# Twelve other weight blocks are streamed through four places, and the work tiles of a step are packed anew (attention with memory and a state space convolution, one core)

## The chip, the cores and the metric

The kernel runs on one core of a Trainium2 chip. The metric is the device time of one execution in microseconds. A kernel is timed in several runs and the median is given. A profile is one further execution with the hardware profiler on. Engines are named as the profile names them: PE (TensorE, matmuls), PEld (its weight loads), DVE (VectorE), ACT (ScalarE), POOL (GpSimd) and SP (SyncE, which here only issues transfers). A "q" behind an engine is its queue of issued transfers.

## The reference, cut to what matters

There are two parts, and the output joins them side by side. Part B is a convolution of a 2048 x 1024 input with kernels that come from a state space model. It runs first and the change does not touch its code. Part A is a recurrent attention over 64 segments of 32 rows, and each segment needs 8 rows of memory that the one before it wrote:

```python
mem = mem0
for s in range(n_seg):
    h = jnp.concatenate([mem, x[:, s * 32:(s + 1) * 32]], axis=1)
    q, k, v = (jnp.einsum('btd,dhe->bhte', h, W) for W in (Wq, Wk, Wv))
    scores = jnp.where(mask, jnp.einsum('bhqe,bhke->bhqk', q, k) * scale, -1e9)
    o = jnp.einsum('bhqk,bhke->bhqe', softmax(scores), v)
    o = jnp.einsum('bhte,hed->btd', o, Wo)
    mem = o[:, :8]
    outs.append(o[:, 8:])
```

Model width is 1024, with 32 heads of 128. So Wq, Wk, Wv and Wo have 1024 x 4096 elements each, in bf16, 8 MB a matrix, and every segment uses all of them.

## The kernel before

The loop over segments is a chain: the memory rows of one step enter the matmuls of the next. A step works with 32 rows, the 8 rows of memory and 24 rows of x ("hT", transposed). The projections of the other 8 rows of each segment do not depend on memory; they are made ahead of the loop, kept in HBM (PKd, PVd and VXd) and read in by each step (`load_pk`, line 327, and `load_vx`, line 333, which also brings the 24 rows of x of the next step).

**Weights.** The 32 MB of weights are cut in 64 blocks of 128 x 2048 elements, 0.5 MB each. A block is named by matrix, half of the heads and the slice of the contraction, such as ("v", 1, 5), or for Wo by a pair of heads, such as ("o", 9). The on-chip memory (SBUF) holds 49 of them for the whole loop ("resident"). Three ("kept": k 0 7, q 0 7, o 15) lie wholly or half in PSUM and are copied by DVE to SBUF work space in each step (`fetch`, line 292). The other twelve are listed in STREAM and STREAM_O (lines 25 and 26). They are copied once to HBM tiles of their own (WD) and are loaded again in every step, through four places ("wst") used in turn. `unit` (line 261) is called as PE's matmuls are written down: when it meets a streamed block, `stage` (line 294) issues the load on SP's queue to the next of the four places. That load waits until PE has used the block that was loaded four loads earlier. Resident blocks whose first use lies in the first step are loaded from the same queue as they are met.

**A step** in PE's order is: k half 0 (slices 0, 2, 4, 6, 1, 3, 5, 7), q half 0, k half 1 with the transposes of k0 and q0 and the first scores in between, q half 1, v half 0 with the transposes of k1 and q1 after three of its slices and the second scores at its end, v half 1 with the first part's weighted values (pv) after six slices, Wo 0 to 4, pv of the second half, Wo 5 to 15, and the transposes of the new memory rows. Line 365 is the projection matmul (four of 512 columns a block, in four row groups at once), 474 the one with Wo (eight of 256 columns), 376 the transposes, 390 and 394 the scores, 573 the transpose of the new memory, which DVE copies to hT (line 575).

ACT copies each projection from PSUM to SBUF (`evac`, line 371), fills the scores with the mask (384), takes Exp (410), and issues the loads of pk and vx and the two stores of a step's result (`stores`: line 343 to the scratch tensor OLd, 347 to the output). DVE does the softmax sums and the KT0 copy (489), POOL adds the columns of the precomputed keys to KT0 and KT1 (379).

**Work tiles.** All work tiles of a step lie in one SBUF tile, the arena, of 5984 bytes a partition, at byte offsets written by hand (AT, line 36). Tiles that overlap must not live at once. Where they do in part, the framework finds the overlap and puts in a wait: a writer waits for the last readers and writers of what it overwrites, and for a transfer's landing where that is one of them. A step's result ("ob", 1024 bytes) is written by ACT at the step's end, read by the two stores, and its place is written again by the next step. The order of the instructions on each engine is the order in which the program writes them; there is no scheduler in this part.

Of the kernel before, what the change touches and what calls it, by code (L numbers as in the profile page):

```python
# [21 lines left out]

STREAM = {("k", 0): (2, 3), ("q", 0): (4,), ("k", 1): (3,), ("q", 1): (4,), ("v", 0): (0, 6), ("v", 1): (1, 5)}
STREAM_O = (1, 5, 9)

BANK = {("k", 0): "b0", ("q", 0): "b1", ("k", 1): "b2", ("q", 1): "b0", ("v", 0): "b3", ("v", 1): "b2"}
KEPT = {("k", 0, 7): (("K7a", 0, 512), ("K7b", 512, 512), ("K7c", 1024, 512), ("K7d", 1536, 384), (None, 1920, 128)),
# [3 lines left out]
SLOTS = 4  # L33

ARENA = 5984
AT = {"K7a": 4960, "K7b": 2048, "K7c": 1024, "K7d": 3136, "ob": 3904, "pk": 0, "vx": 3392, "Q7a": 2048, "Q7b": 4960,
      "k0": 1024, "q0": 2048, "KT0": 4704, "QT0": 1024, "k1": 1024, "q1": 4288, "pn0": 5312, "pt0": 2304, "KT1": 1024,
      "QT1": 4288, "pb0": 4288, "V0": 1024, "L0": 5472, "o0": 2368, "V1": 1024, "pn1": 2048, "pt1": 4288, "pb1": 0,
      "lb1": 4960, "ln1": 320, "lt1": 0, "L1": 2048, "o1": 3904, "Oa": 4960, "Ob": 2560}


def weight_blocks(Wq, Wk, Wv, Wo):
# [15 lines left out]
def streamed_keys():  # L58
    return [key for key in [(m, t, kc) for (m, t), kcs in STREAM.items() for kc in kcs] + [("o", u) for u in STREAM_O]]

# [172 lines left out]
def part_a(ctx, tc, x, src, WD, HE, seg_len, out_a, ahead, W_res, rest, places, first):  # L233
# [25 lines left out]
    between = {}  # L259
# [22 lines left out]
    def at(name, *dims):  # L282

        n = int(np.prod(dims))
        t_ = arena[:, AT[name] // 2:AT[name] // 2 + n]
        if len(dims) == 1:
            return t_
        names = "abc"[:len(dims)]
        return t_.rearrange("p (%s) -> p %s" % (" ".join(names), " ".join(names)), **dict(zip(names, dims)))

    def words(out, in_):
        nc.vector.tensor_scalar(out=out.bitcast(I32), in0=in_.bitcast(I32), scalar1=0, scalar2=None, op0=ALU.bitwise_or)  # L292

    def stage(key, in_):
        t_ = wst.tile([128, 2048], BF16, name="wst", tag="w%d" % (loads[0] % SLOTS))
        loads[0] += 1
        nc.sync.dma_start(out=t_[:].rearrange("e (h d) -> e h d", h=2) if len(in_.shape) == 3 else t_[:], in_=in_)
        return t_

    def load_kept(key):  # L300
        t_ = first.pop(key) if key in first else stage(key, src(key))
        kept[key] = {}
        for n in (1,) if key in HALF else (0, 1):
            kept[key][n] = ps_k.tile([128, 512], F32, name="keep", tag="keep%d" % sum(len(b) for b in kept.values()))
            words(kept[key][n][:], t_[:, 1024 * n:1024 * n + 1024])
        if key in HALF:
            t_ = ahead.low["half"] if key[0] == "q" else wres.tile([128, 1024], BF16, name="Whalf")
            nc.sync.dma_start(out=t_[:], in_=src(key)[:, 0, :] if key[0] == "o" else src(key)[:, 0:1024])
            halves[key] = [(0, 1024, t_)]
# [15 lines left out]
    def load_pk(j):  # L325
        pk = at("pk", 512)
        nc.scalar.dma_start(out=pk, in_=PKd[j])
        return pk

    def load_vx(j):  # L330
        n = 448 if j + 1 < NS else 256
        vx = at("vx", 448)
        nc.scalar.dma_start(out=vx[:, 0:n], in_=VXd[j + 1, :, 0:n])
        return vx
# [17 lines left out]
    load_kept(("k", 0, 7))  # L352
    fetch(("k", 0, 7))
    pk = load_pk(0)
    between["q", 0, 4] = lambda: load_kept(("q", 0, 7))
    between["v", 0, 6] = lambda: load_kept(("o", 15))
    for s in range(NS):
        def quads(m, t, kcs, a=None):
# [10 lines left out]
        def evac(a, name):  # L369
            q = at(name, 512)  # L370
            nc.scalar.copy(out=q, in_=a[:])  # L371
            return q
# [39 lines left out]
        def weigh(sc, i, pn):  # L412
            x, m_ = flat(sc, i), maxima(i)
            nc.vector.tensor_reduce(out=m_, in_=x, axis=AX.X, op=ALU.add)  # L414
            nc.vector.reciprocal(out=m_, in_=m_)
            pn = at(pn, x.shape[1], NK)
            nc.vector.tensor_tensor(out=pn, in0=x, in1=bc(m_.unsqueeze(2), [128, x.shape[1], NK]), op=ALU.mult)
            return pn

        def turn(pn, pt):  # L420
            n = pn.shape[1]
            pt = at(pt, n + n // 4, SL)
            nc.vector.transpose(out=pt[:, 0:n, :], in_=pn[:, :, 0:SL])
            nc.vector.transpose(out=pt[:, n:n + n // 4, :], in_=pn[:, :, SL:NK])  # L424
            return pt
# [9 lines left out]
        def left_blocks(lt, lk, name):  # L435
            L = at(name, 2, 16, XL)
            nc.gpsimd.tensor_tensor(out=L[:, 0].rearrange("p (a b) k -> p a b k", a=4), in0=bc(lt[:, :, 0:XL].unsqueeze(2), [128, 4, 4, XL]),  # L437
                                    in1=bc(BD[:].unsqueeze(1).unsqueeze(3), [128, 4, 4, XL]), op=ALU.mult)
            spread_l(nc.gpsimd, L[:, 1], lk[:, 0:XL], 0, 16, XL)
            return L  # L440
# [17 lines left out]
        def evac_o(p, name):  # L458
            o = at(name, 4, 4, SL)
            nc.scalar.copy(out=o, in_=p[:].rearrange("p a (g q) -> p a g q", g=4))  # L460
            return o
# [16 lines left out]
        k0 = evac(a, "k0")  # L478
# [3 lines left out]
        q0 = evac(a, "q0")  # L482
# [5 lines left out]
        QT0, KT0 = at("QT0", 4, 4, SL), at("KT0", 4, 4, NK)  # L488
        nc.vector.tensor_copy(out=KT0[:, :, :, 0:SL], in_=pk_[:])  # L489
        nc.scalar.copy(out=QT0, in_=pq[:])  # L490
        vx = load_vx(s)
# [5 lines left out]
        k1 = evac(a, "k1")  # L497
# [3 lines left out]
        pt0 = turn(weigh(sc0, None, "pn0"), "pt0")  # L501
        q1 = evac(a, "q1")
# [5 lines left out]
        KT1, QT1 = at("KT1", 4, 4, NK), at("QT1", 4, 4, SL)  # L508
# [20 lines left out]
        pb0 = at("pb0", 4, 4, SL)  # L529
        spread(pb0, pt0[:, 0:4, :])  # L530
        L0 = left_blocks(pt0[:, 4:8, :], pt0[:, 9, :], "L0")
# [4 lines left out]
        V0 = evac(a, "V0")  # L536
# [7 lines left out]
        o0 = evac_o(pv0, "o0")  # L544
        pt1 = turn(weigh(sc1, 0, "pn1"), "pt1")
        pb1 = at("pb1", 4, 4, SL)
        spread(pb1, pt1[:, 0:4, :])
        lb1 = at("lb1", 512)
        spread_l(nc.vector, lb1.rearrange("p (a k) -> p a k", k=SL), pt1[:, 4, :], 0, 16, SL)
        quads("v", 1, range(6, KC), a)  # L550
        V1 = evac(a, "V1")
# [6 lines left out]
        o1 = evac_o(pv1, "o1")  # L558
        lt1 = turn(weigh(sc1, 1, "ln1"), "lt1")
        oproj(pp[:, 1, :], range(5, 8), o0)  # L560
        L1 = left_blocks(lt1[:, 0:4, :], lt1[:, 4, :], "L1")
        fetch(("o", 15))
        oproj(pp[:, 1, :], range(8, 16), o1)
        ob = at("ob", 2, 256)
# [14 lines left out]
        if s + 1 < NS:  # L579
            pk = load_pk(s + 1)  # L580
# [806 lines left out]
def kernel(  # L1387
# [92 lines left out]
    with ExitStack() as ctx_a:  # L1480
        part_a(ctx_a, tc, A_x[0], src, WD, A_Wo.shape[0] * A_Wo.shape[1], seg_len, out_a, ahead, W_res, rest, places, first)
# [35 lines left out]
```

## Time and profile before

| | us |
|---|---|
| median of 3 runs (lowest, highest) | 2136.48 (2134.81, 2144.58) |
| the profiled execution, its own time | 2141.16 |
| its span | 2139.4 |
| PE busy (share of the span) | 1885.6 (88%) |
| DVE busy | 1442.0 (67%) |
| ACT busy | 1045.2 (49%) |
| POOL busy | 435.8 (20%) |
| mean rate of transfers | 276 GB/s, 590.78 MB |
| streamed blocks, loads of 512 KB | 768 |

Times of the profile are microseconds from the span's start. A row of the page with digits cuts the span in 40 equal slices of 53.5 us, each digit the busy share in tenths. A wait is given as the waiting engine and line, and what released it. "L365 PE MATMUL acc<-wst,a_hT" is the matmul of line 365 that reads a streamed block, "acc<-W,a_hT" one with a resident block; "arena" is any work tile. In a timeline, a bracket at the end of a line is the idle time of the engine ahead of it and what ended that.

### The profile page before, as it was taken

How to read it: one execution, taken by the hardware profiler on the slowest of the kernel's cores; microseconds unless marked ns; L12 is line 12 of the kernel's file. 1: busy time of each engine (PE TensorE's matmuls, PEld its weight loads, DVE VectorE, ACT ScalarE, POOL GpSimd, SP SyncE). 2: the span in 40 equal slices, each digit the busy share in tenths (PEclk: the TensorE clock that was granted, in tenths of full speed). 3: DMA queues.
4: the chain of work that ended last, by engine and by line, in shares of the span. 5: the costliest groups of instructions: out<-in, count | busy, mean ns of one | idle time of the engine just before them, and what ended most of it. 6: DMA issues, size and time to landing. Idle time of an engine off the chain costs nothing. (4 is left out here: it accounts for less than half of the span.)

```text
span 2139.4 us, 78633 instructions
## 1 busy us (share of the span) xinstructions
PE 1885.6 (88%) x33734; PEld 1183.7 (55%) x33734; DVE 1442.0 (67%) x3353; ACT 1045.2 (49%) x1915; POOL 435.8 (20%) x780
## 2 busy tenths in 40 slices
PE   1589999977999779999999999999998998999999
PEld 1365656656888535555555555555554555555554
DVE  8589999989999246566566665666655565666650
ACT  6699999971333324444444444444434343444430
POOL 2145445452111101111111111111111111111121
PEclk9999999989999889999999999999999999999999
DMA  6767886556745899999999999999998999999991
GB/s 162 191 198 229 241 226 176 163 174 204 242 134 175 302 350 328 324 324 338 319 337 333 325 322 324 328 335 338 324 321 302 320 323 317 308 334 334 327 335 57
DMA packets 344019, 590.78 MB, mean 276 GB/s; under 512 B 108537, under 2 KB 220185, under 8 KB 341621
## 3 DMA queue, kind: packets, MB, share of 16 engines
q1 hardware_dynamic: 297016, 528.00, 74.1%
q0 software_dynamic: 10544, 33.69, 4.6%
q10 hardware_dynamic: 36108, 24.07, 3.7%
q8 instruction: 264, 4.33, 0.8%
q14 instruction: 87, 0.70, 0.1%
HBM read 530.86 MB, written 65.26 MB: 279 GB/s over the span
## 5 line engine op out<-in xcount | busy, mean ns | idle before, releaser
L365 PEld LDWEIGHTS <-a_hT 128*32 128x32 bf16 x12352 | 337.5, 96 | 326.5 <-issue 79.6
L371 ACT CAST arena<-acc 128x512 bf16<-128x512 f32 x384 | 224.9, 586 | 421.2 <-PE acc L365 274.6
L365 PE MATMUL acc<-W,a_hT 128*32 128x512 bf16 x4864 | 376.1, 383 | 0.0
L474 PEld LDWEIGHTS <-arena 128*32 128x32 bf16 x8256 | 211.2, 97 | 110.8 <-issue 54.1
L365 PE MATMUL acc<-wst,a_hT 128*32 128x512 bf16 x2304 | 234.3, 385 | 40.2 <-DMA wst<-WD_v 28.9
L292 DVE TENSOR_SCALAR arena<-keep 128x256 int32<-128x256 int32 (+1 forms) x512 | 175.8, 395 | 35.6 <-PE acc L365 31.8
L379 POOL COPY arena<-arena 128x128 bf16<-128x128 bf16 x128 | 37.3, 292 | 720.9 <-PE tr L376 236.5
L474 PE MATMUL pp<-W_o,arena 128*32 128x256 bf16 x4608 | 171.9, 275 | 10.8 <-DMA W_o<-in_A_Wo_dram 6.7
L365 PE MATMUL acc<-MF,a_hT 128*32 128x512 bf16 x2048 | 158.7, 381 | 0.0
L414 DVE TENSOR_REDUCE a_mx<-sc 128x4 f32<-128x160 f32 (+1 forms) x192 | 73.0, 380 | 124.7 <-ACT sc L410 124.7
L167 PE MATMUL pro<-xTl,wsl 128*128 128x512 bf16 x512 | 119.8, 385 | 5.2 <-ACT xTl L111 5.2
L489 DVE COPY arena<-tr 128x512 bf16<-128x512 bf16 x64 | 27.2, 424 | 141.9 <-PE tr L376 96.7
L1050 PEld LDWEIGHTS <-MF 128*128 128x128 bf16 x1024 | 102.6, 101 | 29.9 <-issue 8.6
L410 ACT ACTIVATE sc<-sc 128x160 f32<-128x160 f32 (+1 forms) x192 | 64.2, 334 | 105.0 <-DVE sc L407 100.7
L437 POOL TENSOR_TENSOR arena<-arena,a_BD 128x128 bf16<-128x128 bf16 x128 | 68.5, 535 | 229.8 <-DVE arena L424 212.8
L460 ACT CAST arena<-pv 128x512 bf16<-128x512 f32 x128 | 75.1, 587 | 80.3 <-PE pp L444 59.0
L406 DVE TENSOR_REDUCE a_mx<-sc 128x4 f32<-128x160 f32 (+1 forms) x192 | 71.8, 374 | 59.2 <-PE sc L394 58.1
L567 ACT CAST arena<-pp 128x128 bf16<-128x128 f32 x128 | 27.8, 269 | 163.6 <-PE pp L474 163.6
L1050 PE MATMUL hps<-KT,MF 128*128 128x256 bf16 x720 | 94.1, 283 | 14.7 <-DVE x L1225 11.6
L1282 PE MATMUL yp<-Bt,MI 128*128 128x256 bf16 x680 | 102.8, 273 | 0.8 <-ACT yb L1298 0.8
L1088 ACT ACTIVATE E<-pa 128x648 bf16<-128x648 f32 x128 | 91.3, 713 | 17.9 <-PE pa L1080 14.2
L376 PEld LDWEIGHTS <-arena 128*128 128x128 bf16 x1024 | 57.9, 98 | 75.1 <-issue 37.4
(316 smaller groups left out, 4100.9 us busy)
## 6 DMA issues: line engine op xcount, KB each, us to landing
wst<-WD_v SPq DMA_DIRECT2D x256, 512.0 KB
wst<-WD_k SPq DMA_DIRECT2D x192, 512.0 KB
wst<-WD_o SPq DMA_DIRECT2D x192, 512.0 KB
wst<-WD_q SPq DMA_DIRECT2D x128, 512.0 KB
Ud<-ux POOLq DMA_DIRECT2D x16, 1024.0 KB, 6.0
uq<-Ud SPq DMA_DIRECT2D x32, 512.0 KB
wsl<-in_A_Wk_dram SPq DMA_DIRECT2D x16, 512.0 KB
wsl<-in_A_Wv_dram SPq DMA_DIRECT2D x16, 512.0 KB
```

The lines of the kernel that those rows point to most:

```text
L167: nc.tensor.matmul(a[:], lhsT=w[:, kc, 128 * j:128 * j + 128], rhs=xTl[:, kc, :, :].rearrange("p s k -> p (s k)"), start=(kc == 0), stop=( ...
L292: nc.vector.tensor_scalar(out=out.bitcast(I32), in0=in_.bitcast(I32), scalar1=0, scalar2=None, op0=ALU.bitwise_or)
L365: nc.tensor.matmul(a[32 * g:32 * g + 32, o_:o_ + rhs.shape[1]], lhsT=hT[:, kc, :], rhs=rhs, start=(kc == 0), stop=(kc == KC - 1), tile_pos ...
L371: nc.scalar.copy(out=q, in_=a[:])
L406: nc.vector.tensor_reduce(out=m_, in_=x, axis=AX.X, op=ALU.max)
L414: nc.vector.tensor_reduce(out=m_, in_=x, axis=AX.X, op=ALU.add)
L437: nc.gpsimd.tensor_tensor(out=L[:, 0].rearrange("p (a b) k -> p a b k", a=4), in0=bc(lt[:, :, 0:XL].unsqueeze(2), [128, 4, 4, XL]), in1=bc ...
L460: nc.scalar.copy(out=o, in_=p[:].rearrange("p a (g q) -> p a g q", g=4))
L474: nc.tensor.matmul(po[32 * qt:32 * qt + 32, o_:o_ + rhs.shape[1]], lhsT=oT[:, h % 4, (h % 16) // 4, :], rhs=rhs, start=False, stop=(h == 3 ...
L1050: pe.matmul(s_[r][half][:, cs, :], lhsT=MF[:, kc, 4 * rr + mc, cs, :], rhs=rhs, start=(i == 0 and mc == 0), stop=(i == 1 and mc == 3), ski ...
L1088: sc.activation(out=T["E", r, e // 4][:, lo:lo + 8 * NE].rearrange("p (i c) -> p i c", i=2), in_=T.pop(("p", r, e))[:, :, 0:4 * NE], func= ...
L1282: pe.matmul(yp[:, b, :], lhsT=m_[:, b, cs, kc, :], rhs=Bt[:, kc, j, half, c_, :], start=(kc == 0 and cs == 0 and half == 0), stop=(kc == 3 ...
```

## The change

Twelve blocks are streamed as before, through four places as before, but others: k 0 2, k 0 3, q 1 4, v 0 6 and o 9 remain, and seven are exchanged. In the order of use:

| | before | after |
|---|---|---|
| k 0 | 2, 3 | 2, 3 |
| q 0 | 4 | 5 |
| k 1 | 3 | 5 |
| q 1 | 4 | 4 |
| v 0 | 0, 6 | 2, 6 |
| v 1 | 1, 5 | 3, 6 |
| o | 1, 5, 9 | 3, 9, 11 |

Of the 34 work tiles 14 get another offset. Above all the result ob moves from 3904 to 4960, KT0 from 4704 to 2048, and the pieces of the kept blocks and q0, pb0, o0, pn1, ln1, lt1 and o1 are set around them. The sizes stay. The number of instructions and their order on DVE, ACT and POOL stay, too; on PE the matmuls with streamed and with resident blocks trade places, and on SP the blocks of the loads.

```diff
-STREAM = {("k", 0): (2, 3), ("q", 0): (4,), ("k", 1): (3,), ("q", 1): (4,), ("v", 0): (0, 6), ("v", 1): (1, 5)}
-STREAM_O = (1, 5, 9)
+STREAM = {("k", 0): (2, 3), ("q", 0): (5,), ("k", 1): (5,), ("q", 1): (4,), ("v", 0): (2, 6), ("v", 1): (3, 6)}
+STREAM_O = (3, 9, 11)
...
-AT = {"K7a": 4960, "K7b": 2048, "K7c": 1024, "K7d": 3136, "ob": 3904, "pk": 0, "vx": 3392, "Q7a": 2048, "Q7b": 4960,
-      "k0": 1024, "q0": 2048, "KT0": 4704, "QT0": 1024, "k1": 1024, "q1": 4288, "pn0": 5312, "pt0": 2304, "KT1": 1024,
-      "QT1": 4288, "pb0": 4288, "V0": 1024, "L0": 5472, "o0": 2368, "V1": 1024, "pn1": 2048, "pt1": 4288, "pb1": 0,
-      "lb1": 4960, "ln1": 320, "lt1": 0, "L1": 2048, "o1": 3904, "Oa": 4960, "Ob": 2560}
+AT = {"K7a": 3072, "K7b": 1024, "K7c": 2048, "K7d": 4192, "ob": 4960, "pk": 0, "vx": 3392, "Q7a": 2048, "Q7b": 3072,
+      "k0": 1024, "q0": 3328, "KT0": 2048, "QT0": 1024, "k1": 1024, "q1": 4288, "pn0": 5312, "pt0": 2304, "KT1": 1024,
+      "QT1": 4288, "pb0": 4448, "V0": 1024, "L0": 5472, "o0": 2048, "V1": 1024, "pn1": 3072, "pt1": 4288, "pb1": 0,
+      "lb1": 4960, "ln1": 0, "lt1": 704, "L1": 2048, "o1": 3936, "Oa": 4960, "Ob": 2560}
...
-    between["q", 0, 4] = lambda: load_kept(("q", 0, 7))
+    between["q", 0, 5] = lambda: load_kept(("q", 0, 7))
```

The last line keeps the load of q 0 7 at the same place of the queue, ahead of the streamed block of q half 0.

## The prediction

> **What bounds the kernel now.** I read the page first: TensorE's busy row, the DMA row and the transfer rate.
>
> ```profile
> PE   1589999977999779999999999999998998999999
> DMA  6767886556745899999999999999998999999991
> GB/s 162 191 198 229 241 226 176 163 174 204 242 134 175 302 350 328 324 324 338 319 337 333 325 322 324 328 335 338 324 321 302 320 323 317 308 334 334 327 335 57
> ```
>
> From the 14th slice on (about 717 us) PE and the DMA engines are both at nine tenths. This is the loop of part A. The first writes of the state hT (DVE line 575) date its steps: 775.4 us to 2058.2 us is 62 steps in 1282.8 us, **20.69 us a step**. The rest, 2141.2 − 1282.8 = 858 us of the profiled execution, is the first step, part B ahead of it and the last step with its tail. The change reorders there equal numbers of equal loads, so I set it at zero, with ±2 us for the first step, which waits for 0.5 MB loads in turn.
>
> Then the busy time by stretch, one stretch a step. The columns are length, busy us by engine, clock, DMA share, GB/s.
>
> ```profile
> 857.72:878.99 21.27, 19.15 (x426) 11.04 (x425) 12.50 (x40) 8.68 (x22) 2.85 (x7) 1.00 0.95 315
> 878.99:898.92 19.93, 19.10 (x426) 10.95 (x425) 12.70 (x39) 8.96 (x22) 2.94 (x7) 1.00 0.94 322
> 1309.77:1330.13 20.36, 19.00 (x426) 11.11 (x425) 12.37 (x39) 8.89 (x22) 2.85 (x7) 1.00 0.96 333
> 1392.02:1411.28 19.26, 18.76 (x426) 11.02 (x425) 12.49 (x39) 8.88 (x22) 3.00 (x7) 1.00 0.98 349
> ```
>
> Steps run from 19.26 to 23.12 us with the same work, PE busy about 19.1 in nearly all. So PE's work gives a floor near 19.3 us and waits make the rest. DMA is close behind: the mean over the steps is 6.73 MB at a share of 0.94, so 0.94 × 20.69 = 19.5 us of transfer time a step. The waits of PE in the loop (engine, line, releaser: total us, times, longest):
>
> ```profile
> PE acc L365 <- DMA wst<-WD_v: 26.2, 45, 2.0
> PE tr L376 <- ACT arena L371: 15.9, 25, 1.7
> PE pp L474 <- DMA wst<-WD_o: 12.3, 26, 1.2
> PE tro L573 <- ACT arena L567: 11.1, 57, 0.2
> PE sc L390 <- DVE arena L489: 6.7, 12, 1.2
> ```
>
> Row 4 is untouched. Rows 1 and 3 (with 3.4 us for q and k blocks, 42 us in all) are streamed blocks that come late, rows 2 and 5 come from the packing. The timelines of PE, DVE and ACT show one of each:
>
> ```profile
> 1302.90 0.40 PE L365 MATMUL acc<-wst,a_hT 128*32 128x512 bf16 x4 [1.03 <-DMA wst<-WD_v]
> ...
> 1316.05 0.42 DVE L489 COPY arena<-tr 128x512 bf16<-128x512 bf16 x1 [3.32 <-DMA OLd<-arena]
> ...
> 866.48 0.33 ACTq L333 DMA_DIRECT2D arena<-VXd  x1
> 866.90 0.58 ACT L371 CAST arena<-acc 128x512 bf16<-128x512 f32 x1 [3.49 <-DMA out_dram<-arena]
> ...
> 867.54 0.40 PE L376 MATMUL tr<-a_ident,arena 128*128 128x128 bf16 x4 [0.85 <-ACT arena L371]
> ```
>
> **Part 1, the packing.** No instruction is added or removed on DVE, ACT or POOL. What changes is who waits for the two stores of a step's result. Before, the result lies at 3904 to 4928 and meets KT0 (from 4704) and vx (to 4288). So the two KT0 writes (DVE 489, POOL 379) wait for the store to OLd, and the load of vx (line 333) waits for the store to the output. ACT runs in order: behind that load stand the k1 evacuation, Exp of the first scores and the q1 evacuation, and PE's transposes of k1 and q1 wait for these. After, the result lies at 4960 to 5984. KT0 (2048 to 3328) and vx (3392 to 4288) miss it; the first writers that meet it are the q1 evacuation (4288 to 5312) and pn0 (from 5312). The order of the built program with its waits confirms this. vx then waits only for a block that PE has already used, and POOL's part of KT0 for q0's last matmul: its 0.29 us copy then runs beside eight transposes and twelve matmuls of PE (1.3 us), so it costs nothing; without them it would add 0.3 us a step. The new waits of L1's writes for older matmuls of Wo, and of pn0 for the output store, fall on DVE and POOL, which PE did not wait for there (0.7 us in the loop, on DVE 429).
>
> The worth: I split 61 whole steps by PE's waits. 37 show neither row 2 nor row 5 and average 20.35 us; 24 show one and average 21.21. They also show less waiting for blocks (0.46 against 0.87 us), since a stalled PE lets transfers catch up, so this difference is net of that. If all steps become like the 37: 24 × 0.86 = **−20.6 us**.
>
> What stays: the q1 evacuation starts 8.40 us after the step's start and PE wants its transpose at once, so a store landing later than that still stops PE. The issue of vx, which waits for that store, shows the landings: 5.1 to 9.6 us, 10 of 62 above 8.40, 5.9 us in sum. **+5.9 us**.
>
> Here a rule speaks against the change. The Trainium skill, "DMA: Bandwidth & Descriptors", section Queues, rings and completion order, says that each DMA engine takes turns between the queues with work, a packet at a time. So the stores land late because SP's blocks run with them, and a stream with fewer gaps makes them later. The row: in the step above the output store of 64 KB was issued at 858.3 and landed by 866.5, 8.2 us, with 4 KB rows of the stream beside it. In the new order blocks 9 and 11 of Wo are used 0.43 us apart, so two loads are issued together about 2 us ahead of the stores, where before they were 1.4 us apart. By the row as it stands the cost is 5.9 us; were the rule worth one microsecond on every landing, it would be 19.4 us. I take half a microsecond, 11.9 us, because about a third of one block's transfer (19.5 / 12 = 1.6 us) more lies ahead of the stores: **+6 us** more.
>
> **Part 2, the stream.** Twelve blocks of 0.5 MB as before, through four places; a load is issued when the block four earlier has been used (about 0.45 us for its four matmuls). Positions of use in an unstalled step, us: before 0.45, 1.31, 2.82, 4.99, 7.25, 8.11, 10.10, 11.11, 12.15, 14.26, 15.46, 16.83. The time from issue to use is shortest for the ninth, v1 block 5: 12.15 − 7.25 − 0.45 = 4.45 us. That block alone has 21 of the 42 us, in 31 waits, mean 0.7. After, at 0.215 us a block: 0.45, 1.31, 3.04, 5.42, 7.25, 8.54, 10.10, 11.54, 13.23, 14.70, 16.83, 17.26. The ninth now has 5.53 us, and the shortest is the last, o block 11, with 17.26 − 11.54 − 0.45 = 5.27. Taking 0.8 us off each of the 31 waits leaves 4.7 of 21.4: −16.6 us. But a stream at 0.94 to 0.98 of its time is limited by its rate. A block asked for earlier also queues behind more, and two blocks 0.43 us apart (9 and 11) want 1 MB nearly at once. I let two thirds come back as waits at o block 11 and its neighbours: **−5.5 us** net. From below: all comes back, 0. From above: all 42 us go, but then the step meets the DMA: 20.35 × 0.95 / 0.98 = 19.7 us (0.98 is the best share of any step).
>
> The same page, section Bandwidth, sets the rate of one core that streams alone (425 GB/s in its largest measured transfer) above its share of the memory when both cores of a pair stream (about 358). With 425 my estimate of the floor is 6.73 MB / 425 GB/s = 15.8 us, PE alone would bound the loop and all waits could go. The row says 349 GB/s at a share of 0.98, so 6.73 MB takes 19.3 us. The row decides: there is almost no headroom beyond the best steps.
>
> **Sum.** −20.6 + 5.9 + 6 − 5.5 = −14 us on packing and stream. The removed chain also makes vx earlier (a wait of 0.9 us of PE on it) and Exp of the first scores; both lie beside PE's matmuls: −1. So −15 of 2141.2 us. The profiled execution lies 4.7 us above the median, so from the median: 2136.5 − 15 = **2121 us**.
>
> **Rivals.**
> - *The transfers set the step and waits only move* (chance 0.30): the rows 2 and 5 vanish, but the blocks come as late as before in total. The mean step is then 20.55 to 20.75. Time 2128 to 2140, about 2134. For it: 19.5 us of transfer in 20.69, and stalled steps that wait less for blocks. Against: the 37 steps at 20.35.
> - *Spacing takes the whole gain* (0.15): the steps come to 19.8 to 20.1 us, like the best quarter now, 37 to 55 us less: about 2092. For it: steps of 19.3 to 19.5 exist, with 345 to 349 GB/s. Against: in most steps the same share carries less.
> - *Slower: the stores land later and stop the q1 evacuation* (0.13). Nothing else may yield there: ACT is in order, and new_sc and PE's transposes stand behind it. Adding d to each seen landing, the excess over 8.40 us is 19.4 us at d = 1.0, 29.5 at 1.4, 48.5 at 2.0, 67.2 at 2.5. The gain to be eaten is 20.6 + 5.5 + 1 = 27, so it turns slower at d of about 1.3, by over 0.5% (11 us) at about 1.7, and d = 2 gives 2136.5 − 27 + 48.5 = 2158. Against: stores and stream share the engines now as well, and the landings spread over only 4.5 us.
> - *The packing doesn't do what it says* (0.02): some other overlap keeps a store wait at KT0. The program's listed waits show none.
>
> **How the numbers follow.** The forecast, 2105 to 2127, has 0.40. With the large gain 0.15; no change 0.30 (a third of it at 2126 to 2130, on the edge); slower 0.13 and 0.02. 0.5% is 10.7 us, about what a measurement of this kernel can tell from no change. Faster than 2125.8: 0.38 + 0.15 + 0.03 = 0.56. Slower than 2147: 0.13. The rest, 0.31, is within. The range 2094 to 2144 leaves out half of the large gain and most of the slower case. The forecast's own range is 2105 to 2127.
>
> **What would show it.** Right: no PE wait on DVE 489 and no ACT wait on the output store ahead of k1's evacuation; a k1 evacuation always 6.7 us into the step; the ninth block's wait mostly gone and o block 11 the new worst; mean step 20.4 us. Wrong: waits of the q1 evacuation on the output store in more than 20 steps (rival 3), or a total wait for blocks above 55 us (rival 1), or under 20 us (rival 2).

## The result, and the profile after

| | before | after |
|---|---|---|
| median of 22 runs each, us (lowest, highest) | 2137.57 (2126.88, 2149.57) | 2126.74 (2115.72, 2137.56) |
| ratio, 95% interval | | 0.9945 (0.9927 to 0.9963) |
| span of the profiled execution, us | 2139.4 | 2124.5 |
| the 62 steps of the loop, us (one step) | 1282.8 (20.69) | 1267.2 (20.44) |

The ratio is 11.8 us less (7.9 to 15.6), the medians differ by 10.8. In the profiled executions the loop gives 15.6 us and the rest of the program takes 0.7 us more, so the change lies in the loop alone. The page after, with its busy digits of PE and DMA and the rates in 40 slices:

```profile
PE   1589999977999779999999999999999999999989
DMA  6767786566735799999999999999999999999991
GB/s 163 186 197 236 220 242 188 150 187 179 265 124 194 280 334 337 337 328 332 327 338 337 335 318 333 337 333 317 330 323 330 330 328 323 325 331 331 324 342 50
```

The picture is the same, two full rows, with a rate a little higher. The busy time of two steps in turn (length, PE, PEld, DVE, ACT, POOL, clock, DMA share, GB/s):

```profile
856.35:877.45 21.10, 19.36 (x426) 11.01 (x425) 12.40 (x39) 8.89 (x22) 2.87 (x7) 1.00 0.95 326
877.45:896.70 19.25, 18.73 (x426) 11.05 (x425) 12.51 (x39) 8.90 (x22) 2.86 (x7) 1.00 0.97 341
```

Long steps are still there. What PE waits for in the loop, however, has changed. The rows of waits, here and in the experiments, cover 800 to 2050 us of a profile, as those in the prediction do:

```profile
PE acc L365 <- DMA wst<-WD_q: 22.5, 27, 2.1
PE pp L474 <- DMA wst<-WD_o: 15.3, 28, 1.6
PE pp L474 <- ACT arena L460: 8.8, 40, 0.5
PE tr L376 <- ACT arena L371: 7.5, 13, 0.9
PE acc L365 <- DMA wst<-WD_v: 3.2, 9, 0.9
...
PE sc L390 <- POOL arena L379: 1.4, 2, 1.2
```

The blocks of v, 26.2 us before, are down to 3.2, and the transposes from 15.9 to 7.5. The wait for KT0's copy on DVE is gone. In their place stands a block of q, at 22.5 us. A smaller wait has grown, too: that of Wo's matmuls for ACT's copy of the second half's values (o1, line 460), which before was:

```profile
PE pp L474 <- ACT arena L460: 3.7, 15, 0.3
```

PE's and ACT's timelines of the first of the two steps above show the wait for q:

```profile
860.37 0.40 PE L365 MATMUL acc<-wst,a_hT 128*32 128x512 bf16 x4 [0.81 <-DMA wst<-WD_q]
...
862.44 0.59 ACT L490 COPY arena<-tr 128x512 bf16<-128x512 bf16 x1
862.45 0.33 ACTq L333 DMA_DIRECT2D arena<-VXd  x1
864.02 0.59 ACT L371 CAST arena<-acc 128x512 bf16<-128x512 f32 x1 [0.99 <-PE acc L365]
```

The load of vx is issued at once behind line 490, and the evacuation of k1 waits for PE alone. PE itself stands still for 0.8 us, until 4.0 us into the step, for the streamed block of q half 0. All streamed blocks together make PE wait 43.7 us, as before (43.5, counted alike over the 62 steps), so the waits have moved from v1 block 5 (21.1 us to nothing; its successor, v1 block 6, has 1.8) to q 0 block 5 (0.9 us for its forerunner, 22.5 now) and o block 11 (11.6; o block 9, the last one before, had 8.4).

### The profile page after: what moved, and what is told of

It reads as the page before. It is cut to its first block, busy times and chain, and to the rows that moved or that the text cites. A ratio compares the mean times of both kernels' runs of the same rounds, so it can differ in the third digit from the quotient of the medians.

```text
span 2124.5 us, 78567 instructions
## 1 busy us (share of the span) xinstructions
PE 1881.1 (89%) x33734; PEld 1183.0 (56%) x33734; DVE 1436.0 (68%) x3353; ACT 1048.8 (49%) x1915; POOL 431.3 (20%) x780
## 5 line engine op out<-in xcount | busy, mean ns | idle before, releaser
L365 PE MATMUL acc<-W,a_hT 128*32 128x512 bf16 x4864 | 363.6, 382 | 0.4 <-issue 0.4
L365 PE MATMUL acc<-wst,a_hT 128*32 128x512 bf16 x2304 | 231.9, 383 | 36.3 <-DMA wst<-WD_q 22.5
L474 PE MATMUL pp<-W_o,arena 128*32 128x256 bf16 x4608 | 186.2, 276 | 16.2 <-ACT arena L460 9.3
L437 POOL TENSOR_TENSOR arena<-arena,a_BD 128x128 bf16<-128x128 bf16 x128 | 73.1, 571 | 242.7 <-DVE arena L424 226.1
L1050 PE MATMUL hps<-KT,MF 128*128 128x256 bf16 x720 | 94.5, 284 | 14.4 <-DVE x L1225 11.4
L474 PE MATMUL pp<-wst,arena 128*32 128x256 bf16 x1536 | 76.9, 276 | 18.6 <-DMA wst<-WD_o 17.3
```

The costliest lines, as they stand in the source:

```text
L365: nc.tensor.matmul(a[32 * g:32 * g + 32, o_:o_ + rhs.shape[1]], lhsT=hT[:, kc, :], rhs=rhs, start=(kc == 0), stop=(kc == KC - 1), tile_pos ...
L474: nc.tensor.matmul(po[32 * qt:32 * qt + 32, o_:o_ + rhs.shape[1]], lhsT=oT[:, h % 4, (h % 16) // 4, :], rhs=rhs, start=False, stop=(h == 3 ...
L1050: pe.matmul(s_[r][half][:, cs, :], lhsT=MF[:, kc, 4 * rr + mc, cs, :], rhs=rhs, start=(i == 0 and mc == 0), stop=(i == 1 and mc == 3), ski ...
```

## The experiments

My theory was the prediction's: most of the gain comes from the stores' waits, and the stream mostly moves its waits. Rivals: spacing carries the gain; the rate of the transfers bounds the step and nothing gains; and loads issued together hold up the stores. All ratios are to the kernel before, measured on the same chip at the same time; they can differ by some us from the quotient of the two medians. Waits given in the text are sums over the 62 steps from PE's timelines.

**1. The packing alone.** The new AT with the old twelve blocks:

```diff
-AT = {"K7a": 4960, "K7b": 2048, "K7c": 1024, "K7d": 3136, "ob": 3904, "pk": 0, "vx": 3392, "Q7a": 2048, "Q7b": 4960,
-      "k0": 1024, "q0": 2048, "KT0": 4704, "QT0": 1024, "k1": 1024, "q1": 4288, "pn0": 5312, "pt0": 2304, "KT1": 1024,
...
+AT = {"K7a": 3072, "K7b": 1024, "K7c": 2048, "K7d": 4192, "ob": 4960, "pk": 0, "vx": 3392, "Q7a": 2048, "Q7b": 3072,
+      "k0": 1024, "q0": 3328, "KT0": 2048, "QT0": 1024, "k1": 1024, "q1": 4288, "pn0": 5312, "pt0": 2304, "KT1": 1024,
...
```

> The kernel before with the new packing alone, the old twelve blocks. My theory (the stores' waits are the larger part of the gain): the waits of KT0 and of k1's evacuation go, v1 block 5 stays the worst block with 20 us or more; ratio 0.993 to 0.995, some 11 to 15 us. Rival (a faster PE only meets the transfers, the spacing is what counts): ratio 0.998 to 1.000, and the waits for blocks grow from 42 to over 55 us.

Measured: 2115.56 us, ratio 0.9873 (0.9831 to 0.9914), 27 us less (21 by the medians). That is more than I expected and more than the whole change gives. PE's waits in the loop:

```profile
PE acc L365 <- DMA wst<-WD_v: 27.7, 61, 2.6
PE pp L474 <- DMA wst<-WD_o: 6.9, 17, 1.1
PE tr L376 <- ACT arena L371: 4.9, 5, 2.4
...
PE pp L474 <- ACT arena L460: 3.0, 16, 0.2
```

Scores wait 0.5 us for KT0 (6.7 before), transposes 4.9 (15.9), and blocks 38.9 (43.5): the freed time was not eaten by the transfers, so the rival that predicts that falls for the packing. The run moves all 14 tiles at once; which of them carry the gain is read from the waits, not tested one by one.

**2. The stream alone.** The new twelve blocks with the old packing:

```diff
-STREAM = {("k", 0): (2, 3), ("q", 0): (4,), ("k", 1): (3,), ("q", 1): (4,), ("v", 0): (0, 6), ("v", 1): (1, 5)}
-STREAM_O = (1, 5, 9)
+STREAM = {("k", 0): (2, 3), ("q", 0): (5,), ("k", 1): (5,), ("q", 1): (4,), ("v", 0): (2, 6), ("v", 1): (3, 6)}
+STREAM_O = (3, 9, 11)
```

> The kernel before with the new twelve blocks alone, the old packing. My theory: v1's late block vanishes and q half 0 block 5 and o block 11 take its place; ratio 0.997 to 1.000. Rival (spacing carries the gain): ratio 0.994 to 0.996 with waits for blocks under 35 us. The waits on the stores stay in both, and grow if loads issued together delay the stores: over 23 us for KT0 and the transposes.

Measured: 2173.36 us, ratio 1.0152 (1.0103 to 1.0202), 32 us **slower**. Neither theory had that size; the last clause had the direction.

```profile
PE sc L390 <- DVE arena L489: 29.2, 31, 2.1
PE tr L376 <- ACT arena L371: 25.6, 38, 1.6
PE acc L365 <- DMA wst<-WD_q: 17.3, 27, 1.5
```

The first two are the waits on the stores. Over all 62 steps they are 33.6 us for KT0, POOL's part included, and 25.6 for the transposes, against 6.7 and 15.9: 36.6 us more, while the blocks are waited for 8.7 us less (34.8 against 43.5). (The profiled execution took 2182.5 us, 9 us above the median, so the rows overstate the loss.) The issue of vx, which follows the output store's landing, comes 7.9 us into the step on average (6.8 before, and up to 11.3 where it was 9.6). The transfers' packets in the traces agree: the last packet of the two stores ends 7.4 us into the step on average, 6.3 before. So the stores land later, by a microsecond on average.

**3. Block 7 of Wo in place of 9**, in the kernel after:

```diff
-STREAM_O = (3, 9, 11)
+STREAM_O = (3, 7, 11)
```

> The kernel after, with o block 7 streamed in place of o block 9. The load of q half 0 block 5 is issued when o block 9 (now 7) has been used, so its time from issue to use grows from about 5.1 to 6.0 us. If the reuse distance makes the wait: q 0 5's 22.5 us fall below 8, and with nothing given back the ratio to before is 0.988 to 0.991. If the transfers' rate makes it: the wait turns up at other blocks, the sum stays 35 to 45 us, ratio 0.993 to 0.996 as after.

Measured: 2103.78 us, ratio 0.9828 (0.9783 to 0.9872), below both kernels. The wait of q 0 5 falls from 22.5 to 2.1 us, all blocks from 43.7 to 31.6, and the transposes from 7.5 to 1.9.

```profile
PE pp L474 <- DMA wst<-WD_o: 21.5, 44, 1.7
...
PE acc L365 <- DMA wst<-WD_q: 4.6, 7, 1.3
...
PE tr L376 <- ACT arena L371: 1.9, 4, 0.7
```

(The row of q also has q 1 4 and the last step, which lies behind the 62.) One load issued some 0.9 us earlier is worth 23 us against the kernel after (2126.74 to 2103.78, measured at different times), and 11.8 us against the packing alone, measured with it. So the time from issue to use counts, though it was not the one that I had picked out. The edit also parts the two loads that blocks 9 and 11 set off together; this run does not tell the two effects apart.

**4. q1 off the result.** The kernel after with q1 elsewhere:

```diff
-"q1": 4288
+"q1": 2048
```

> The kernel after, with q1 at 2048 in place of 4288, so that its evacuation no longer meets the result whose output store may still run. If that store stops PE through the q1 evacuation: the 7.5 us of PE's transposes waiting for line 371 go to under 1, and the ratio to before is 0.990 to 0.993. If the freed time only meets the transfers: the 7.5 us turn into waits for blocks, ratio 0.994 to 0.996. A wait of pn0 on the same store (DVE) may show, at no cost.

Measured: 2203.09 us, ratio 1.0292 (1.0238 to 1.0347). This experiment was badly made. At 2048 q1 covers pt0 (2304 to 2944), which DVE has yet to use, so the first half's attention weights are overwritten and its values are computed from wrong numbers; and the evacuation now waits for DVE to write pt0:

```profile
ACT arena L371 <- DVE arena L424: 127.5, 58, 3.7
PE tr L376 <- ACT arena L371: 70.8, 58, 2.1
```

It says nothing on the store's wait. It does show the price of one bad overlap: the transposes wait 1.2 us in each step, 75.9 us over the loop and 68 more than in the kernel after, of the 76 us by which it lies above that kernel.

**5. Half of the bytes.** From the second step on the kernel after loads 256 KB of each block and its matmuls read that half twice, which leaves out the other half of these weights; the number of loads, the places and the matmuls stay:

```diff
-        return stage(key, WD[key][:])
+            nc.sync.dma_start(out=t_[:, 0:1024], in_=WD[key][:, 0:1024])
+            return [(0, 1024, t_), (1024, 1024, t_)]
```

> The kernel after with half of each streamed block loaded from the second step on (128 x 1024, 256 KB), and its matmuls reading that half twice, so part of the weights is wrong and all of the work, its loads, places and order are kept. If the transfers are what still bounds the step: the waits for blocks and for the stores go to nearly nothing and the step falls to PE's own 19.3 us, about 2050 to 2060 us in all. If PE's own chain or the late stores bound it: 2090 us or more.

Measured: 2048.99 us, ratio 0.9563 (0.9537 to 0.9589), step 19.18 us. The loop in one stretch:

```profile
775.00:1964.50 1189.50, 1156.89 (x26351) 679.52 (x26350) 769.79 (x2419) 551.07 (x1241) 176.96 (x434) 1.00 0.63 190
```

The only wait of PE in it that exceeds 1 us in sum:

```profile
PE pp L479 <- ACT arena L465: 13.7, 61, 0.5
```

With the DMA share at 0.63 PE's waits for blocks, stores and KT0 sum to under 1 us; what is left is the wait for the copy of o1 (line 465 of this kernel), 0.2 us a step. So PE's chain with its compute engines is 19.2 us a step, and what lies above it in the kernel after goes when the transfers are halved: the blocks directly, the stores through the packing.

**6. vx later.** The kernel before with one load moved in ACT's order:

```diff
-        vx = load_vx(s)
...
         q1 = evac(a, "q1")
+        vx = load_vx(s)
```

> The kernel before with the load of vx moved in ACT's order behind the evacuation of q1, nothing else: ACT no longer stands behind that load's wait on the output store when k1 is to be evacuated. If that queueing is the larger part of the packing's worth: PE's transposes stop waiting for line 371 but for the store to OLd through q1, and the ratio is 0.991 to 0.995; KT0's wait of 7 us stays. If KT0's wait is the larger part, or the time only meets the transfers: 0.997 to 1.001.

Measured: 2157.16 us, ratio 1.0079 (1.0060 to 1.0099), slower. (Its profiled execution took 2142.8 us, the shortest of its runs, so the rows understate it.)

```profile
PE acc L365 <- DMA wst<-WD_v: 43.7, 58, 1.9
PE pv L448 <- DMA arena<-VXd: 14.0, 21, 1.7
...
PE tr L376 <- ACT arena L371: 1.8, 3, 0.7
```

The queueing on ACT was what held the transposes: 15.9 us fall to 1.8. But both theories missed what the moved load does. It goes out 8.7 us into the step in place of 6.8, nearer to v1 block 5 (whose wait grows from 21.1 us to 40.2), and reaches pv late (14 us). Here a transfer of 112 KB at another moment cost more than the queueing saved. The packing gets the first without the second, since there vx goes out at 5.2 us.

**7. A more even stream.** The kernel of run 3, with k 1 4, v 0 1 and 5, v 1 2, and o 2 as well:

```diff
-STREAM = {("k", 0): (2, 3), ("q", 0): (5,), ("k", 1): (5,), ("q", 1): (4,), ("v", 0): (2, 6), ("v", 1): (3, 6)}
-STREAM_O = (3, 7, 11)
+STREAM = {("k", 0): (2, 3), ("q", 0): (5,), ("k", 1): (4,), ("q", 1): (4,), ("v", 0): (1, 5), ("v", 1): (2, 6)}
+STREAM_O = (2, 7, 11)
```

> The kernel with o block 7, with k 1 4, v 0 1 and 5, v 1 2 and 6 and o 2, 7 and 11 streamed: the shortest time from issue to use grows from 5.27 to 5.48 us, o block 7's from 5.35 to 5.56 and k 0 3's from 5.46 to 5.68. If the shortest reuse still makes the waits: those of o 7, o 11, k 3 and o 3 (28 us in that kernel) fall by 6 us or more and the ratio to before is 0.978 to 0.981. If the rate of transfers bounds it by now: 0.982 to 0.985, no different.

Measured: 2102.53 us, ratio 0.9816 (0.9789 to 0.9844), no different from run 3. The named waits fall by about 7 us (27 to 20, with o 2 for o 3), as the first theory said, but other blocks wait longer: the sum is 32.2 us (31.6 there). So the first theory's waits came and its time did not. The ratio lies between the two forecasts; the sum speaks for the rival of the rate.

**8. pk behind the stores**, in the kernel of run 3:

```diff
-            pk = load_pk(s + 1)
...
             stores(s, ob)
+            pk = load_pk(s + 1)
```

> The kernel with o block 7, with the load of pk (128 KB) issued on ACT's queue behind the two stores in place of ahead of them. If what lies ahead of the stores sets their landing: they land about 0.8 us earlier, and the evacuations that wait for the output store nearly vanish; but pk lands later, POOL's part of KT0 with it, and PE's scores wait for POOL: slower, ratio 0.984 to 0.990, as pk is the tighter of the two. If pk has room: 0.979 to 0.982.

Measured: 2279.62 us, ratio 1.0624 (1.0576 to 1.0672). The direction was expected, the size was not.

```profile
POOL arena L379 <- DMA arena<-PKd: 477.9, 52, 12.6
...
PE sc L390 <- POOL arena L379: 127.5, 53, 5.7
```

The scores wait 141 us over the loop for pk, up to 5.7 us in a step, since POOL's part of KT0 waits until it has landed behind the two stores. This is not all of the 180 us by which the loop is longer than in run 3. The two loops, this run first:

```profile
774.62:2198.70 1424.08, 1229.09 (x26351) 708.35 (x26350) 775.38 (x2419) 548.99 (x1241) 172.99 (x434) 0.95 0.85 293
776.31:2019.91 1243.60, 1176.64 (x26351) 685.60 (x26350) 771.48 (x2418) 551.76 (x1241) 178.07 (x434) 1.00 0.96 335
```

The same matmuls keep PE busy for 52 us more, at a mean granted clock of 0.95 in place of 1.00. The clock was below full in 32 of the 62 steps. These took 24.5 us on average with 3.2 us of the scores' wait, the others 21.3 with 1.3. So long waits and a lower clock come together here, and the ratio holds both; what lowered the clock was not tested.

**9. Block 7 for 9 with the old packing**, to test whether the two loads together delayed the stores in run 2 (edit against the kernel of run 2):

```diff
-STREAM_O = (3, 9, 11)
+STREAM_O = (3, 7, 11)
```

> The kernel before with the new twelve blocks, o block 7 in place of 9, and the old packing. If the two loads that o blocks 9 and 11 set off together delayed the stores (landing a microsecond later in the run of the stream alone, KT0's wait 33.6 us and the transposes' 25.6): the stores land as before the change, KT0's wait is under 15 us, the transposes' under 18, and the ratio is 0.995 to 1.002. If any stream without gaps delays the stores: the waits stay above 20 us each and the ratio is 1.008 to 1.016.

Measured: 2133.89 us, ratio 0.9972 (0.9955 to 0.9989), by the ratios 38 us less than run 2. (The profiled execution took 2126.4 us, 7 us below the median, so the rows flatter it.)

```profile
PE sc L390 <- DVE arena L489: 9.6, 13, 1.6
PE tr L376 <- ACT arena L371: 7.1, 16, 1.1
```

KT0's wait is 11.0 us over the whole loop (33.6 in run 2), the transposes' 7.1 (25.6), vx goes out at 6.8 us and the stores' last packet ends at 6.2, both as before the change. One block exchanged, and the delay is gone: it is the two loads set off together ahead of the stores that made it.

**10. A quarter of the output store.** The kernel after stores 16 of 64 KB to the output in each step but the last (three quarters of the attention's output stay unwritten):

```diff
-            nc.scalar.dma_start(out=rows, in_=ob[:, 0, :])
+            nc.scalar.dma_start(out=rows[0:1], in_=ob[0:32, 0, :])
```

> The kernel after, storing only the first quarter of each step's result to the output (32 x 256, 16 KB in place of 64), so three quarters of the attention's output are left unwritten but for the last step. If the small transfers between q half 0 block 5's issue and its use are what makes that block late: its 22.5 us fall below 14, the transposes' 7.5 us go to under 3 as the store lands early, and the ratio is 0.986 to 0.991. If its reuse distance alone makes it: the 22.5 us stay within 4, and the ratio is 0.992 to 0.995.

Measured: 2114.67 us, ratio 0.9892 (0.9861 to 0.9922).

```profile
PE acc L365 <- DMA wst<-WD_q: 16.4, 27, 2.0
```

q 0 5's wait is 14.0 us of it, on the edge of the first theory's bound, and the transposes' is 0. So the output store alone makes over a third of that block's lateness; the rest is the distance, pk and the other store together. 48 KB less a step are worth some 11 us against the kernel after.

## Why the prediction was right in sum and wrong in its terms

The predicted median was 2121 us and the forecast −15; the ratio gives −11.8. That the sum came out is luck: the packing was undervalued and the new blocks were misjudged the other way. The prediction has −15.7 for the packing (−20.6, +5.9 and −1) and +0.5 for the blocks (+6 and −5.5). Measured are −21 (medians) or −27 (ratio) for the packing alone and +10 or +16 for the blocks on top of it. The terms:

- **The loop and nothing else**: right, 15.6 us in the loop and 0.7 the other way outside it. The step was forecast at 20.4 us and is 20.44.
- **Packing, −20.6 for the removed stalls, +5.9 for stores that still stop q1**: right in mechanism, too small. Alone it gives −27 (−36 to −18; −21 by the medians). KT0's wait shrinks by 6.2 us and the transposes' by 11.0; the 4.9 us left there answer to my 5.9. Blocks wait 4.6 us less, where my split of the steps had them wait more once the stalls are gone (0.87 against 0.46 us a step). The load of vx, priced at −1, is a candidate for that: in run 6 a later one went with longer waits for v1 block 5. (Row 4 of the waits before, line 573, goes from 11.4 us to nothing, but hardly its time: from the last Wo matmul to that transpose it is 0.68 us before and 0.64 in run 1.)
- **Later stores, +6**: the weighed rule of the Trainium skill ("DMA: Bandwidth & Descriptors", section Queues, rings and completion order), that each DMA engine takes turns between the queues, points the right way; the runs show the delay, not the turns. Its one microsecond, which I halved, is what they show: after two loads issued together vx goes out 1.06 us later in run 2, and the stores' last packet ends at 7.2 us in the changed kernel against 6.2 in run 1. The cost was smaller than forecast: the transposes wait 7.5 us for evacuations in the changed kernel, 4.9 in run 1, so 2.6 us and not 6. What I did not see is that the new blocks need the new packing: with the old one, the later stores reach PE through KT0 as well. So the packing is worth 47 us with the new stream (2173.36 to 2126.74, medians measured at different times) and 21 to 27 with the old.
- **Stream, −5.5**: wrong in sign, and the step that failed. With the new packing the new blocks cost 2126.74 − 2115.56 = 11 us by medians measured at different times (ratios: 0.9945 / 0.9873 = 1.0073, 16 us), later stores included. In the profiled executions it is 10.4 us, and PE's waits show where: 4.8 us more at blocks (38.9 to 43.7), 2.6 at the transposes and 6.0 at the copy of o1 (3.0 to 9.0). The prediction says that "the shortest is the last, o block 11, with 17.26 − 11.54 − 0.45 = 5.27". I did not carry the positions over the step's border. The third block of a step takes the place of the second last block of the step ahead: 3.04 + 19.3 − 16.83 − 0.45 = 5.06 us, the shortest of all, and in that stretch run pk and the two stores. It waits 22.5 us, and so all that v1 block 5 gave up (21.1) comes back there, not two thirds of it and elsewhere. Run 3 moves the freeing use by 0.9 us and those 22.5 become 2.1. The copy of o1 was put at nothing. In the changed kernel's 11 steps in which a block of v1 or of Wo 0 to 4 came late, PE stood idle for 0.02 us on average ahead of Wo 8, the first that needs o1; in the other 51 it was 0.19. So part of what a late block cost had hidden another wait, which appears when the block is in time. (One position is misread: before, o block 5 is used at 15.8 us and not at 15.46, behind pv; no term changes by it.)
- **The ninth block's wait**: expected mostly gone, 21.1 us to 1.8. Right. **q1's evacuation waiting for the output store in more than 20 steps** was the sign of the slower rival: it is 8 (of 62), so that rival did not come with the new packing. With the old one it did, through KT0. **No wait on DVE 489, and none on the output store just ahead of k1's evacuation**: right (12 and 21 before). **k1's evacuation always 6.7 us into the step**: wrong, it starts at 6.7 to 10.5, 7.3 on average, since q 0 5 stops PE ahead of it (6.8 on average in run 1). **o block 11 the new worst**: wrong, it is second (11.6 us).
- **The floor**: that PE alone is 19.3 us a step is confirmed by run 5 (19.18). The 19.5 us of the transfers agree with run 7, where a more even stream gains nothing more at steps of 20.06 us and a DMA share of 0.96 (19.3 us), but no run here isolates them.

How a block's wait goes with its time from issue to use. Positions here are those of steps without a wait for blocks, of the new blocks from run 5; waits are sums of 62 steps:

| block, kernel | us from issue to use | wait, us |
|---|---|---|
| v1 5, before / run 1 | 4.45 | 21.1 / 17.5 |
| q0 5, after / run 2 / run 10 | 5.02 | 22.5 / 17.6 / 14.0 |
| o 11, after / run 3 | 5.15 | 11.6 / 10.8 |
| o 5, before / run 1 | 5.23 | 4.3 / 1.7 |
| o 9, before / run 1 | 5.27 | 8.4 / 3.7 |
| o 7, run 3 | 5.36 | 6.7 |
| o 11, run 7 | 5.36 | 9.5 |
| v1 6, after / run 3 | 5.37 | 1.8 / 0 |
| o 3, after / run 3 | 5.39 | 2.9 / 4.1 |
| k0 3, after / run 3 | 5.66 | 2.7 / 5.4 |
| v1 1, before / run 1 | 5.67 | 1.4 / 8.0 |
| q0 5, run 3 | 5.86 | 2.1 |

The two shortest distances have the longest waits. Between 5.1 and 5.7 us the waits run from 0 to 12 without a clear order, and the same block at the same distance can wait 1.4 us in one kernel and 8.0 in another. So the distance is not all: what else is under way counts.

Left open: how much of q0 5's lateness is pk and how much the store to OLd (run 10 cut the output store alone), and how much of what run 3 gains at it is the time and how much the parting of the two loads; and what a free q1 would be worth, since run 4 did not free it. The last 53 us between run 7 (2102.5) and half of the bytes (2049.0) go with the bytes; how much of them is the transfers' rate, and how far a better order of the small ones would eat into them, was not tried. Nor was the wait for the copy of o1 taken away in any run. The version to keep is that of run 3 or run 7, the packing with block 7 for 9: 0.9828 (0.9783 to 0.9872) or 0.9816 (0.9789 to 0.9844).

## What to carry to other kernels

Where a loop streams through a few places, write down for every load the time from the use that frees its place to its own use, around the loop's border as well, and look at which small transfers fall into the shortest. Here two loads set off together just ahead of a store delayed that store by a microsecond, which is cheap only if no tile of the next stage lies on what is being stored. When a late transfer is mended, expect a part of the gain to go to the wait that it had hidden. And the two halves of a change like this can't be judged apart: the stream here is a loss of 32 us with one packing and of 11 with the other, and with block 7 of Wo in place of 9 it is a gain of 6 or of 12.

## What the runs showed of the hardware that was not expected

- A store of 64 KB beside a stream of 512 KB loads took 8.2 us to land in the step shown in the prediction, and by the issue of vx behind it up to 9.0 us before the change and 10.4 in run 2. With loads of half that size (run 5) the stores' last packet ended 3.7 us behind the issue of the output store on average, in the kernel after 6.6. A 128 KB load issued behind two such stores made its user wait up to 5.7 us (run 8).
- In the first step loads of 512 KB that PE waited for one after another came every 1.35 us (388 GB/s, from the starts of the Wo matmuls). By the rows of the profile before, the stretch from 762 to 774 us moved 396 GB/s at a DMA share of 1.05 and the loop 325 GB/s at 0.94. For the same busy time of the DMA engines the loop's mix thus carries about a twelfth less; whether its small transfers make that was not measured.
- In run 8, where PE waits longest, the granted clock fell below full in 32 of the 62 steps, and PE's busy time in the loop rose by 52 us; in the profile of every other run here it did so in at most 4 steps.
